# A fused attention and gated-convolution kernel: gate and value weights from one transposed h, token loads for two chunks, finer pieces and a new order

## The chip, the cores and the metric

The kernel runs on one core of a Trainium2 chip. The metric is the device time of one execution in microseconds (us), lower is better. Engines are named as in the profile: PE (TensorE; PEld its weight loads), DVE (VectorE), ACT (ScalarE), POOL (GpSimd), SP (SyncE, which here issues nearly all DMAs).

## What is computed

Two functions in a row, on x of 4 batches x 12800 tokens x 128 channels, all float32 outside:

```python
def mab(q, kv):
    s = scale * (q @ kv.transpose(0, 2, 1))
    a = softmax(s)              # with 1e-9 added to the sum
    return a @ kv
h = mab(inducing, x)            # 32 rows per batch
y = mab(x, h)                   # every token again: y = p @ h, p is tokens x 32

for k in range(5):              # causal convolution along the tokens, per channel
    gate_pre += conv_w[k] * y_shifted[k]
gate = 1 / (1 + exp(-gate_pre))
out = (gate * (y @ w_val)) @ w_out
```

Since y = p @ h, the kernel never forms y. The gate's sum over taps becomes matmuls of p (32 rows, shifted by k tokens) with the weights h * conv_w[k], and the value branch a matmul of p with h @ w_val. So each batch needs, before its gates, a stationary operand W: 5 tap weights and 1 value weight, each 32 rows (of h) x 128 channels, four times one below the other (for the four strips), in two float16 halves (high, and the rest).

## The kernel before

A batch's 12800 tokens are four strips of 3200, which stand on the four quarters of the 128 partitions. A strip is cut into seven chunks of some 500 tokens (SIZES). The work of a batch is a chain of stages:

- load_xt loads a chunk with channels on the partitions (xt). load_xk loads it with tokens on the partitions and a column of ones (xk). In batch 0 make_xk makes the xk of every chunk (MADE) on chip instead: PE transposes blocks of 128 x 128 (L315), ACT or DVE evicts them (L112, L114).
- s1 (L335): scores against the inducing rows; DVE evicts them with a running maximum (L351). gmax takes the maximum over the strips (L363, L387, four operations of 32 partitions at L373, on POOL or DVE). e1: exp on ACT (L395), transposition on DVE (L400). h (L419): the sum over tokens on PE, gathered in H (L436 to L440). prep (L454 to L462): h divided by its sum, with channels on the partitions: hT, 128 x 32.
- prep2 and prep3 make W: the conv taps times hT on POOL with channels on the partitions (cg at L487, wf at L488), halves by ACT and POOL (L492, L493), the value row h @ w_val on PE (L782) and its halves on DVE (L508, L509); then 24 small PE transposes for each half (L527), which put each piece of 32 rows into its quarter, and a copy of 768 columns by ACT or DVE (L112, L114).
- s2 (L590) and joint: the second scores of one or two chunks (JOINT), transposed by DVE (L601), maximum (L613), subtraction on POOL (L619), exp on ACT (L625), sum and reciprocal on DVE (L631 to L634), scaling on POOL (L642), transposition back (L647), and the halves P1 (ACT, L653) and P2 (POOL, L661).
- visit: the gate matmuls of a chunk (L676) run together with the value matmuls of the chunk before (L685); tanh on ACT (L747), the product on DVE (L756), halves on ACT and POOL (L768, L773); outp (L782) multiplies by w_out, eviction by ACT or DVE (L817, L815), store by SP (L822).

All these are operations of a plan. They are numbered as they are made, and TURN is the order, written out by hand, in which they are issued: each engine runs its own operations in that order, SP its loads and stores too. MOVED lists the operations that go to their other engine, BANK the PSUM bank of each PE tile, FULL the output matmuls that use the whole array. Buffers are rings of BUFS tiles: 10 for xt, 4 for xk; a load waits in SP's queue until its tile is free. The weights come as 64-bit numbers (w64, L187) and are turned into float32 by eleven operations on DVE (L199 to L212).

In TURN, batch 0 begins with the loads of chunk 0, then 1, 2, 4, 3, the weights, 6 and 5. After its hT come s1 of batch 1's first chunks, s2 and W of batch 0, the gates of chunk 0, then s1 and h of batch 1 among the gates of batch 0.

Of the kernel before, what the change touches and what calls it, by code (L numbers as in the profile page):

```python
# [19 lines left out]
P = 128  # L20
# [64 lines left out]
def tile_kernel(ctx: ExitStack, tc: tile.TileContext, xt, xk, indT_in, w64, out):  # L85
# [71 lines left out]
    def f_const():  # L157
# [3 lines left out]
        ident = const.tile([P, P], F16, name="ident")  # L161
        make_identity(nc, ident)
# [6 lines left out]
        c_.update(ident=ident, identf=identf, pick=pick)  # L169
# [186 lines left out]
    def gmax(b, g):  # L356
# [109 lines left out]
    def prep2(b):  # L466

        key, w2, gmx, vmx = ("ps", "pv", b), ("w2", b), ("gmx", b), ("vmx", b)
        wf, cg = ("wf", b), ("cg", b)
# [5 lines left out]

        def g0():
            gm = sb(pb, gmx, [P, 1])
# [4 lines left out]
            st["gs", b] = gs  # L482

        i = op("DVE", g0, [ix["hT", b], iw], [gmx], [("hT", b)])
# [6 lines left out]
        ig = op("POOL", g1, [i], [wf, cg], [("hT", b)])  # L491
        ih = op("ACT", lambda: S.copy(sb(pw, w2, [P, 2, TAPS + 1, M], F16)[:, 0, :TAPS], st[wf]), [ig], [w2], [wf])  # L492
        il = op("POOL", lambda: G.tensor_tensor(st[w2][:, 1, :TAPS], st[wf], st[w2][:, 0, :TAPS], ALU.subtract),  # L493
                [ih], [], [wf, w2])

        def g2():
# [5 lines left out]
            st["vs", b] = vs  # L502

        i = op("DVE", g2, [i4], [vmx], [key])
# [6 lines left out]
        iv = op("DVE", g3, [i, ih], [], [key, w2])  # L511
        ix["w2", b] = [[ih, iv], [il, iv]]
# [6 lines left out]

    def prep3(b, e):  # L520
        key, w2, W = ("ps", "wt", b, e), ("w2", b), ("W", b)

        def f6():
            t = pt(key).bitcast(F16)[:, :(TAPS + 1) * P].rearrange("p (k c) -> p k c", c=P)
            for q in range(TAPS + 1):
                for r in range(R):
                    T.transpose(t[32 * r:32 * r + 32, q, :], st[w2][:, e, q, :], c_["ident"])  # L527

        i6 = PE(f6, ix[w2][e], [key], [w2], "strips")

        def f7(j=len(plan.ops)):
            if e == 0:
                sb(pb, W, [P, 2, TAPS + 1, P], F16)
            copy(j, st[W][:, e], st[key].bitcast(F16)[:, :(TAPS + 1) * P].rearrange("p (k c) -> p k c", c=P))

        i7 = op("DVE" if e == 0 else "ACT", f7, [i6] + ([ix[W]] if e else []), [W] * (1 - e), [key] + [W] * e,
                alt="ACT" if e == 0 else "DVE")
        ix[W] = ix["W", b, e] = i7
# [462 lines left out]
```

## Time and profile before

| | |
|---|---|
| three runs | 280.59, 278.68, 280.46 us; median 280.46 |
| the profiled execution | 278.53 us, its span 276.4 us |
| PE busy | 95% of the span |
| DVE, ACT, POOL busy | 82%, 71%, 70% |
| DMA | 73.48 MB, mean 266 GB/s |

The profile is of one execution. The span runs from its first to its last instruction; the time of the execution is a little longer. A busy PE is not PE at its peak, since the ends of pipelined matmuls are modelled.

### The profile page before, as it was taken

What the parts mean: (1) busy time and instruction counts of PE and PEld (TensorE: products, weight loads), DVE (VectorE), ACT (ScalarE), POOL (GpSimd) and SP (SyncE); (2) the same over time, 40 slices, a digit from 0 to 9 for tenths busy, and PEclk for the clock granted to TensorE, in tenths of its full rate; (3) what the DMA queues carried; (4) which work ended last, traced back from release to release, by engine and by line L of the source; (5) the groups of instructions that cost most, each with busy time, mean ns of one, the idle gap of its engine ahead of it and who ended that gap; (6) DMA issues with size and microseconds to landing.
All of it is one profiled execution on the core that took longest, in us unless ns stands there. A gap on an engine that the chain in (4) does not pass through costs nothing.

```text
span 276.4 us, 10872 instructions
## 1 busy us (share of the span) xinstructions
PE 263.7 (95%) x4655; PEld 142.3 (51%) x4655; DVE 227.6 (82%) x441; ACT 196.2 (71%) x257; POOL 194.4 (70%) x152
## 2 busy tenths in 40 slices
PE   8989987999999999999999999999999999999993
PEld 4567634766434473475454356656353445443551
DVE  0688899989999977979999799869979997785680
ACT  2547248696588897875877877858878697887764
POOL 1011068976768895985799739876998898997691
PEclk9999999999999999999999999999999999999999
DMA  7999699799989889659989997633134143344467
GB/s 223 408 408 385 224 409 407 262 364 407 348 275 384 314 284 411 263 198 359 365 272 398 329 384 231 256 129 143 58 114 161 64 169 121 115 162 168 154 231 274
DMA packets 30255, 73.48 MB, mean 266 GB/s; under 512 B 3456, under 2 KB 12800, under 8 KB 30208
## 3 DMA queue, kind: packets, MB, share of 16 engines
q1 hardware_dynamic: 30064, 72.79, 71.9%
q8 instruction: 36, 0.59, 0.9%
q14 instruction: 11, 0.09, 0.1%
q10 hardware_dynamic: 144, 0.02, 0.0%
HBM read 46.57 MB, written 26.21 MB: 263 GB/s over the span
## 4 chain that ended last, share of the span: by engine, by line
PE 57%; DVE 16%; DMA 12%; ACT 4%; issue 4%; POOL 3%; SPq 1%; DVEq 0%; ACTq 0%; POOLq 0%
PE banks L676 20%; PE banks L782 17%; PE banks L419 6%; PE banks L590 5%; DMA xt<-in_xt_dram 4%; PE banks L685 4%; DVE tg L756 4%; PE banks L335 3%; DMA raw<-in_w_dram 3%; DMA xk<-in_xk_dram 2%; DMA out_dram<-os 2%; PE banks L315 2%; DVE e L601 2%; ACT os L817 2%; DVE os L815 2%
## 5 line engine op out<-in xcount | busy, mean ns | idle before, releaser
L773 POOL TENSOR_TENSOR gl<-tg,gh 128x1024 f16<-128x1024 f32 (+4 forms) x54 | 106.2, 1972 | 26.3 <-PE banks L782 12.5
L676 PE MATMUL banks<-P,W 32*128 32x512 f16 (+5 forms) x1680 | 105.5, 352 | 1.3 <-ACT W L112 1.0
L676 PEld LDWEIGHTS <-W 32*128 32x128 f16 x1680 | 54.3, 92 | 38.2 <-issue 8.6
L747 ACT ACTIVATE tg<-banks,gsc 128x1024 f32<-128x1024 f32 (+5 forms) x56 | 55.3, 1018 | 22.6 <-PE banks L676 21.4
L756 DVE SCALAR_TENSOR_TENSOR tg<-tg,banks 128x1024 f32<-128x1024 f32 (+5 forms) x56 | 60.5, 1096 | 5.7 <-PE banks L685 4.9
L782 PE MATMUL banks<-gh,wo 128*32 128x448 f16 (+6 forms) x642 | 61.6, 359 | 0.8 <-DVE tg L756 0.6
L768 ACT CAST gh<-tg 128x1024 f16<-128x1024 f32 (+4 forms) x54 | 52.0, 969 | 10.3 <-DVE tg L756 9.3
L782 PEld LDWEIGHTS <-wo 128*32 128x32 f16 (+1 forms) x963 | 31.8, 97 | 38.5 <-issue 14.8
L685 PE MATMUL banks<-P,W 32*128 32x512 f16 (+5 forms) x336 | 41.7, 353 | 2.3 <-ACT tg L747 1.5
L815 DVE TENSOR_SCALAR os<-banks,osc 128x448 f32<-128x448 f32 (+4 forms) x49 | 32.4, 688 | 11.0 <-PE banks L782 9.5
L782 PE MATMUL banks<-gl,wo 128*32 128x448 f16 (+7 forms) x321 | 40.2, 358 | 0.0
L817 ACT ACTIVATE os<-banks,osc 128x512 f32<-128x512 f32 (+4 forms) x57 | 34.9, 646 | 7.5 <-PE banks L782 6.1
L642 POOL TENSOR_TENSOR e<-e,z 128x1024 f32<-128x1024 f32 (+7 forms) x17 | 25.0, 1468 | 7.1 <-ACT tg L747 2.2
L661 POOL TENSOR_TENSOR P<-pt,P 128x1024 f16<-128x1024 f32 (+7 forms) x17 | 27.9, 1640 | 1.8 <-ACT P L653 1.7
L619 POOL TENSOR_TENSOR e<-e,m 128x1024 f32<-128x1024 f32 (+7 forms) x17 | 24.9, 1470 | 5.4 <-DVE m L613 4.8
L419 PE MATMUL banks<-xk,et 128*32 128x129 f32 x800 | 26.0, 274 | 0.3 <-DVE et L400 0.3
L419 PEld LDWEIGHTS banks<-xk,et 128*32 128x32 f32 x800 | 23.1, 110 | 5.9 <-issue 3.0
L335 PE MATMUL banks<-xt,indT 128*32 128x512 f32 (+5 forms) x224 | 25.1, 557 | 0.0
L590 PE MATMUL banks<-xt,hT 128*32 128x512 f32 (+5 forms) x224 | 24.4, 553 | 0.6 <-ACT tg L747 0.5
L351 DVE TENSOR_SCALAR_CACHE_REDUCE ss<-banks 128x1024 f32<-128x1024 f32 (+8 forms) x17 | 15.9, 933 | 8.6 <-PE banks L335 8.4
L685 PEld LDWEIGHTS <-W 32*128 32x128 f16 x336 | 14.2, 92 | 14.1 <-issue 11.6
L395 ACT ACTIVATE ss<-ss,ng 128x1024 f32<-128x1024 f32 (+8 forms) x17 | 15.5, 922 | 7.0 <-DVE ng L373 6.7
(98 smaller groups left out, 254.4 us busy)
## 6 DMA issues: line engine op xcount, KB each, us to landing
xt<-in_xt_dram SPq DMA_DIRECT2D x28, 512.0 KB, 8.1
xk<-in_xk_dram SPq DMA_DIRECT2D x25, 451.5 KB, 6.8
xt<-in_xt_dram SPq DMA_DIRECT2D x23, 448.0 KB, 7.6
out_dram<-os SPq DMA_DIRECT2D x36, 256.0 KB, 2.9
out_dram<-os SPq DMA_DIRECT2D x40, 224.0 KB, 2.6
xk<-in_xk_dram SPq DMA_DIRECT2D x15, 516.0 KB, 7.0
out_dram<-os SPq DMA_DIRECT2D x20, 240.0 KB, 2.7
out_dram<-os SPq DMA_DIRECT2D x4, 208.0 KB, 4.9
```

What stands on the lines that cost most here:

```text
L335: T.matmul(s[32 * r:32 * r + 32, at:at + n], c_["indT"], st[xkey][:, o:o + n // 32, r, :], start=True, stop=True)
L419: T.matmul(t[32 * s:32 * s + 32, :P + 1], st[et][:, at + 32 * i:at + 32 * i + 32], st[xs[c][0]][:, xs[c][1] + i, :], start=j < R, stop=j > ...
L590: T.matmul(s[32 * r:32 * r + 32, at:at + n], st["hT", b], st[xkey][:, m:m + n // 32, r, :], start=True, stop=True)
L676: T.matmul(two(("ps", "g", b, c, r // 2))[:, r % 2, :n], st["W", b][q, w, k, :], st[("P1", "P2")[e]][q, o:o + n], start=u == 0, stop=u == ...
L685: T.matmul(two(("ps", "v", b, c, r // 2))[:, r % 2, :n], st["W", b][q, w, TAPS, :], st[("P1", "P2")[e]][q, o:o + n], start=u == 0, stop=u ...
L747: S.activation(t[:, :, :n], two(("ps", "g", b, c, p))[:, :, :n], AF.Tanh, scale=st["gsc", b])
L756: V.scalar_tensor_tensor(t, t, 1.0, two(("ps", "v", b, c, p))[:, :, :n], ALU.add, ALU.mult)
L768: S.copy(sb(pw, g1, [P, 2, 512], F16)[:, :, :n], st[tg][:, :, :n])
L773: on(j).tensor_tensor(sb(pw, g2, [P, 2, 512], F16)[:, :, :n], st[tg][:, :, :n], st[g1][:, :, :n], ALU.subtract)
L782: T.matmul(t[q], w[:, q], x, start=j == 0, stop=j == len(terms) - 1)
L815: V.tensor_scalar(o, a, st["osc", b], None, ALU.mult)
L817: S.activation(o, a, AF.Copy, scale=st["osc", b])
```

## The change

- **Weights.** g0 (DVE) also writes hn: hT scaled and repeated four times along the columns, 128 x 128. One PE transpose (tg) turns it, so that h stands on 4 x 32 partitions with channels in the columns. g1 (DVE) multiplies it by cwB, the conv taps spread over all partitions, 640 columns from PSUM; ACT casts the high half straight into W (gh), POOL subtracts for the low half (gl). The value row goes the same way: pn, transpose tv, a copy of 128 columns by ACT, the low half by DVE (g3). cwB is made once: 5 PE transposes of broadcast columns of conv_w, and one ACT copy. prep3 with its 48 small transposes and its copies is gone, and the float16 identity.
- **Batch 0's tokens.** MADE holds five chunks: chunks 5 and 6 of batch 0 come as xk by DMA, 1.06 MB each. GROUPS and PAIRS handle chunks 5 and 6 apart: one more maximum.
- **Pieces.** JOINT of batch 0 cuts chunks 1 and 2 into two pieces each (192 and 224, 256 and 256 columns a strip); a chunk's gates wait for all its pieces.
- **to_strips** writes the strip maximum in three operations instead of four.
- **Order.** TURN, MOVED, BANK and FULL are new. Loads of batch 0 now begin with the first halves of chunks 2 and 3, then 0, 1, the weights, the second halves, 4, 5 and 6, batch 1's first xt, and the token tiles of 5 and 6. The weights' first DVE operation stands ahead of the first s1's eviction. On PE, batch 1's first s1 precedes the last two h of batch 0, batch 1's first h precedes chunk 0's gates and its second precedes chunk 1's gates. In the pieces' order the second of chunk 1 goes first, and the second of chunk 2 is done ahead of the first of chunk 1. Of 10 and 11 maxima, 2 and 7 run on POOL.

```diff
-            for r in range(R):
-                on(j).tensor_scalar(st[ng][32 * r:32 * r + 32, g:g + 1], st[m1][:M, 1:], st[m1][M:2 * M, 1:], -SCALE,
-                                    ALU.max, ALU.mult)
+            to_strips(on(j), st[ng][:, g:g + 1], st[m1], -SCALE)
...
+    def to_strips(e, t, m, by):
+
+        for q in range(2):
+            e.tensor_scalar(t[M * q:M * q + M], m[:M, 1:2], m[M:2 * M, 1:2], by, ALU.max, ALU.mult)
+        e.tensor_copy(t[2 * M:], t[:2 * M])
...
+        def rows(key, x):
+            T.transpose(pt(key)[:, :P], st[x], c_["identf"])
...
+            V.tensor_scalar(sb(pw, hn, [P, P]).rearrange("p (r j) -> p r j", r=R), st["hT", b][:, None, :].broadcast_to([P, R, M]),
+                            gs, None, ALU.mult)
...
         def g1():
-            G.tensor_scalar(sb(pw, cg, [P, TAPS]), c_["cwT"], st["gs", b], 1.0, ALU.mult, ALU.mult)
-            G.tensor_tensor(sb(pw, wf, [P, TAPS, M]), st["hT", b][:, None, :].broadcast_to([P, TAPS, M]),
-                            st[cg][:, :, None].broadcast_to([P, TAPS, M]), ALU.mult)
+            t = sb(pw, wf, [P, 1024])[:, :TAPS * P].rearrange("p (k c) -> p k c", c=P)
+            V.tensor_tensor(t, st[gk][:, None, :P].broadcast_to([P, TAPS, P]), c_["cwB"], ALU.mult)
...
+        def gh():
+            S.copy(st[W][:, 0, :TAPS], st[wf][:, :TAPS * P].rearrange("p (k c) -> p k c", c=P))
...
+        def gl():
+            G.tensor_tensor(st[W][:, 1, :TAPS], st[wf][:, :TAPS * P].rearrange("p (k c) -> p k c", c=P), st[W][:, 0, :TAPS],
+                            ALU.subtract)
...
+            V.tensor_scalar(sb(pw, pn, [P, P]).rearrange("p (r j) -> p r j", r=R), st[key][:, None, :M].broadcast_to([P, R, M]),
+                            vs, None, ALU.mult)
...
+        iv = op("ACT", lambda: S.copy(st[W][:, 0, TAPS], st[vk][:, :P]), [it, i0], [], [vk, W])
 
         def g3():
-            w, p, vs = st[w2], st[key][:, :M], st["vs", b]
-            V.tensor_scalar(w[:, 0, TAPS], p, vs, None, ALU.mult)
-            V.scalar_tensor_tensor(w[:, 1, TAPS], p, vs, w[:, 0, TAPS], ALU.mult, ALU.subtract)
+            V.tensor_tensor(st[W][:, 1, TAPS], st[vk][:, :P], st[W][:, 0, TAPS], ALU.subtract)
...
-    def prep3(b, e):
-        key, w2, W = ("ps", "wt", b, e), ("w2", b), ("W", b)
-
-        def f6():
-            t = pt(key).bitcast(F16)[:, :(TAPS + 1) * P].rearrange("p (k c) -> p k c", c=P)
-            for q in range(TAPS + 1):
-                for r in range(R):
-                    T.transpose(t[32 * r:32 * r + 32, q, :], st[w2][:, e, q, :], c_["ident"])
...
-        cs = JOINT[b][g]
-        ns = [wid(b, c) for c in cs]
+        ps = [(q, 0, wid(b, q) // 32) if isinstance(q, int) else q for q in JOINT[b][g]]
+        cs = [q[0] for q in ps]
+        ns = [32 * (q[2] - q[1]) for q in ps]
...
-                if ix["P", b, c] not in deps:
-                    deps.append(ix["P", b, c])
+                    deps += ix["W", b]
+                deps += [i for i in ix["P", b, c] if i not in deps]
...
+    def cw_tp():
+        t = pt(("ps", "cw"))
+        for k in range(TAPS):
+            T.transpose(t[:, P * k:P * k + P], c_["cwT"][:, k:k + 1].broadcast_to([P, P]), c_["identf"])
...
-GROUPS = [[[0, 1], [2], [3, 4], [5, 6]], [[0, 1, 2], [3, 4, 5, 6]], [[0, 1, 2], [3, 4, 5, 6]], [[0, 1, 2], [3, 4, 5, 6]]]
-PAIRS = [[[0], [1], [2], [3, 4], [5, 6]]] + [[[0], [1, 2], [3, 4], [5, 6]]] * 3
+GROUPS = [[[0, 1], [2], [3, 4], [5], [6]], [[0, 1, 2], [3, 4, 5, 6]], [[0, 1, 2], [3, 4, 5, 6]], [[0, 1, 2], [3, 4, 5, 6]]]
+PAIRS = [[[0], [1], [2], [3, 4], [5], [6]]] + [[[0], [1, 2], [3, 4], [5, 6]]] * 3
 SUMS = [[[c] for c in range(7)]] + [[[0], [1, 2], [3, 4], [5, 6]]] * 3
-JOINT = [[[0], [1], [2], [3, 4], [5, 6]]] + [[[0], [1, 2], [3, 4], [5, 6]]] * 3
-MADE = set(range(7))
+JOINT = [[[0], [(1, 0, 6)], [(1, 6, 13)], [(2, 0, 8)], [(2, 8, 16)], [3, 4], [5, 6]]] + [[[0], [1, 2], [3, 4], [5, 6]]] * 3
+MADE = set(range(5))
...
 TURN = [
...
```

## Rows read from the trace of the kernel before

**Rows 1.** The page, part 1: engine, busy us, share of the span, instructions.

```profile
PE 263.7 (95%) x4655; PEld 142.3 (51%) x4655; DVE 227.6 (82%) x441; ACT 196.2 (71%) x257; POOL 194.4 (70%) x152
```

**Rows 2.** Stretches: us; busy of PE, PEld, DVE, ACT, POOL (instructions); clock, DMA share, GB/s.

```profile
0.00:6.90 6.90, 5.73 (x23) 2.77 (x23) 0.65 (x3) 1.49 (x2) 1.32 (x12) 1.00 0.73 222
6.90:27.60 20.70, 19.34 (x215) 13.16 (x212) 15.57 (x48) 12.26 (x17) 2.25 (x8) 1.00 1.01 401
27.60:34.50 6.90, 6.38 (x180) 4.40 (x178) 6.05 (x18) 1.91 (x3) 0.27 (x1) 1.00 0.66 225
...
30.00:44.50 14.50, 11.21 (x268) 5.86 (x262) 13.49 (x46) 5.35 (x10) 7.25 (x15) 1.00 1.01 383
...
62.00:262.00 200.00, 198.03 (x3526) 100.82 (x3523) 172.88 (x304) 152.94 (x194) 160.64 (x99) 1.00 0.67 244
```

**Rows 3.** The chain that ended last: start us, us, what it ran over.

```profile
19.33 2.84 PE banks L315 x24
22.17 1.85 PE banks L335 x16
...
28.00 3.85 PE banks L419 x128
...
33.23 0.20 DVE hT L462
...
43.47 0.98 POOL P L661
...
44.49 0.27 PE banks L676
...
53.19 1.15 PE banks L782 x45
```

**Rows 4.** Timeline, 32 to 43 us: start, us, engine, line, operation [idle before].

```profile
32.62 0.19 DVE L460 TENSOR_SCALAR zr<-banks 128x32 f32<-128x32 f32 x1
...
40.72 1.63 PE L676 MATMUL banks<-P,W 32*128 32x224 f16 x60 [0.98 <-ACT W L112]
...
41.59 0.61 DVE L647 STREAM_TRANSPOSE pt<-e 128x416 f32<-128x416 f32 x1
...
42.03 1.35 POOL L373 TENSOR_SCALAR ng<-m 32x1 f32<-32x1 f32 x4
```

**Rows 5.** Timeline of SP's DMA issues, 8 to 32 us.

```profile
8.05 11.18 SPq L263 DMA_DIRECT2D xt<-in_xt_dram  x10
29.20 2.82 SPq L283 DMA_DIRECT2D xk<-in_xk_dram  x6
```

**Rows 6.** The chain again, one half of a batch's small weight transposes.

```profile
97.02 0.34 PE banks L527 x24
```

**Rows 7.** Timeline of PE, 0 to 9 us.

```profile
1.17 3.60 PE L831 MATMUL banks<-zero 128*128 128x512 f16 x8 [1.17 <-DVE warm L159]
...
4.56 1.70 PE L315 MATMUL banks<-identf,xt 128*128 128x128 f32 x7
...
6.19 0.90 PE L335 MATMUL banks<-xt,indT 128*32 128x224 f32 x8
...
8.07 0.91 PE L335 MATMUL banks<-xt,indT 128*32 128x416 f32 x8
```

**Rows 8.** Groups by shape: line, engine, operation, shapes, count | busy us, mean ns | idle.

```profile
L756 DVE SCALAR_TENSOR_TENSOR tg<-tg,banks 128x1024 f32<-128x1024 f32 x20 | 23.8, 1209 | 2.4 <-PE banks L685 2.0 <-ACT gh L768 0.4
...
L756 DVE SCALAR_TENSOR_TENSOR tg<-tg,banks 128x448 f32<-128x448 f32 x2 | 1.2, 614 | 0.1
...
L440 DVE TENSOR_TENSOR H<-H,banks 128x129 f32<-128x129 f32 x9 | 2.5, 283 | 3.8 <-PE banks L419 2.7 <-ACT os L817 0.6 <-ACT gh L768 0.2
...
L631 DVE TENSOR_REDUCE z<-e 128x16 f32<-128x512 f32 x2 | 1.4, 679 | 0.0
...
L631 DVE TENSOR_REDUCE z<-e 128x8 f32<-128x256 f32 x1 | 0.4, 408 | 0.0
...
L211 DVE TENSOR_SCALAR ul<-raw 128x261 int32<-128x261 int32 x1 | 0.3, 292 | 0.0
```

More of the change, by code (lines that the diff above doesn't have):

```diff
@@ L481, in g0, with tg @@
             V.reciprocal(gs, gm)
-            st["gs", b] = gs
-        i = op("DVE", g0, [ix["hT", b], iw], [gmx], [("hT", b)])
-        def g1():
-            G.tensor_scalar(sb(pw, cg, [P, TAPS]), c_["cwT"], st["gs", b], 1.0, ALU.mult, ALU.mult)
-            G.tensor_tensor(sb(pw, wf, [P, TAPS, M]), st["hT", b][:, None, :].broadcast_to([P, TAPS, M]),
-                            st[cg][:, :, None].broadcast_to([P, TAPS, M]), ALU.mult)
[L491 to L494, printed above, removed]
+            V.tensor_scalar(sb(pw, hn, [P, P]).rearrange("p (r j) -> p r j", r=R), st["hT", b][:, None, :].broadcast_to([P, R, M]),
+                            gs, None, ALU.mult)
+        i0 = op("DVE", g0, [ix["hT", b], iw], [gmx, hn, W], [("hT", b)])
+        def tg():
+            rows(gk, hn)
+        i = PE(tg, [i0, i_const], [gk], [hn])
+        def g1():
+            t = sb(pw, wf, [P, 1024])[:, :TAPS * P].rearrange("p (k c) -> p k c", c=P)
+            V.tensor_tensor(t, st[gk][:, None, :P].broadcast_to([P, TAPS, P]), c_["cwB"], ALU.mult)
+        i = op("DVE", g1, [i, i_cw], [wf], [gk])
+        def gh():
+            S.copy(st[W][:, 0, :TAPS], st[wf][:, :TAPS * P].rearrange("p (k c) -> p k c", c=P))
+        ih = op("ACT", gh, [i], [], [wf, W])
+        def gl():
+            G.tensor_tensor(st[W][:, 1, :TAPS], st[wf][:, :TAPS * P].rearrange("p (k c) -> p k c", c=P), st[W][:, 0, :TAPS],
+                            ALU.subtract)
+        il = op("POOL", gl, [ih], [], [wf, W])
         def g2():
@@ L553, in f1 @@
             over_strips(on(j), st[qm], TINY)
-            for r in range(R):
-                on(j).tensor_scalar(u[32 * r:32 * r + 32], st[qm][:M, 1:2], st[qm][M:2 * M, 1:2], 1.0 / SO, ALU.max, ALU.mult)
+            to_strips(on(j), u, st[qm], 1.0 / SO)
             on(j).tensor_scalar(sb(pb, ("osc", b), [P, 1]), u, 0.5 / SP, None, ALU.mult)
@@ L585, in f @@
             s = pt(key)
-            for c, n, at in zip(cs, ns, places(ns)):
+            for (c, i0, i1), n, at in zip(ps, ns, places(ns)):
                 xkey, m = xt_of(b, c)
-                m -= HALO // 32 if c == 0 else 0
+                m += i0 - (HALO // 32 if c == 0 else 0)
                 for r in range(R):
@@ L603, in s2, with joint @@
         ix["tin", b, g] = op("DVE", tin, [i], [ek], [key], size=sum(ns))
-        joint(b, g, cs)
-    def joint(b, g, cs):
-        n = sum(wid(b, c) for c in cs)
+        joint(b, g, ps)
+    def joint(b, g, ps):
+        n = sum(32 * (q[2] - q[1]) for q in ps)
+        c0, i0 = ps[0][:2]
+        first = c0 == 0 and i0 == 0
         nb = n // 32
@@ L634, in sm @@
             V.reciprocal(z[:, 0, :nb], w[:, 0])
-            if cs[0] == 0:
+            if first:
                 V.memset(z[:M, 0, :1], 0.0)
@@ L663, in joint @@
         i = op("POOL", lo, [i], [], [qk], size=n)
-        for c in cs:
-            ix["P", b, c] = i
+        for c, _, _ in ps:
+            ix.setdefault(("P", b, c), []).append(i)
     taps = [(k, e, 0) for k in range(TAPS) for e in range(2)] + [(k, 0, 1) for k in range(TAPS)]
@@ L835, in tile_kernel, with cw_ev @@
     iw = weights(op("SP", f_wload, [], [("tg", "w", 0)], size=P * K64 * 8))
+    def cw_tp():
+        t = pt(("ps", "cw"))
+        for k in range(TAPS):
+            T.transpose(t[:, P * k:P * k + P], c_["cwT"][:, k:k + 1].broadcast_to([P, P]), c_["identf"])
+    def cw_ev():
+        c_["cwB"] = const.tile([P, TAPS, P], F32, name="cwB")
+        S.copy(c_["cwB"], st["ps", "cw"][:, :TAPS * P].rearrange("p (k c) -> p k c", c=P))
+    i_cw = op("ACT", cw_ev, [PE(cw_tp, [iw, i_const], [("ps", "cw")], size=TAPS, wide=2)], [], [("ps", "cw")])
     for b in range(B):
@@ L855, in tile_kernel @@
         prep2(b)
-        prep3(b, 0)
-        prep3(b, 1)
         prep_out(b)
```

39 lines of the change are left out of this document (16 added, 23 removed), and 128 rows, old and new, of tables (BANK, MOVED, TURN).

## The prediction

> **What bounds the kernel now.** The page's first part [rows 1] says TensorE: PE is busy 263.7 us of a span of 276.4. Busy time there is not peak rate, so I split the span by stage [rows 2]. From 62 to 262 us PE has 198.0 of 200 us, while DVE has 172.9 and POOL 160.6: in that stretch an instruction taken off PE shortens the kernel. From 30 to 44.5 us it is not so: PE 11.2, DVE 13.5 of 14.5. The start is a third thing: from 6.9 to 27.6 us DMA moves 401 GB/s at a share of 1.01, then drops to 225 GB/s.
>
> So there are three stages with three limits: loading, then DVE, then PE to the end. The chain of waits [rows 3] shows the seams. Around 20 to 32 us it runs over PE: 24 transposes in 2.84 us, s1, h, and at last 128 h matmuls in 3.85 us to 31.85. hT is done at 33.43. From there the chain is almost all DVE, until POOL writes chunk 1's low half of P (43.47 to 44.45) and the gate matmuls of chunk 1 follow at 44.49. The gates of chunk 0 ran at 40.72 for 1.63 us [rows 4], so PE had nothing to do for about two microseconds ahead of 44.49. SP issues nothing from 19.23 to 29.20 us [rows 5]: the token tiles of batch 1 wait for buffers that the h matmuls free.
>
> **The change, part by part.**
>
> *PE instructions.* 32 of the 100 block transposes go (chunks 5 and 6): at 2.84/24 = 0.118 us [rows 3], 3.8 us. The 48 small weight transposes of each batch go: 24 take 0.34 us [rows 6], so 0.68 per batch and 2.7 us in all. Added are 5 transposes of spread conv_w and 2 per batch, 13 in all, 1.5 us at 0.118. Net 5.0 us less PE work. Only batches 1 to 3 lie in the PE stage, with 3 x (0.68 - 0.24) = 1.3 us; that part I count in full. The other 3.7 us lie in the first two stages, where DMA and DVE end last.
>
> *Loading.* Chunks 5 and 6 come twice, as xt and as tokens: 2 x 16 x 66,048 B = 2.11 MB more. Before, all that is issued up to 19.23 us (9.83 MB by the loads' sizes) is in by 27.6 us: 222 GB/s x 6.9 us + 401 x 20.7 gives the same 9.83 MB [rows 2]. In the new order the token tile of chunk 6 ends 9.98 MB: batch 0's xt 6.62, w 0.27, batch 1's first xt 0.98, two token tiles 2.11. It takes the buffer of chunk 2, whose h stands well ahead in PE's order, so the queue need not stop: moved by 28.0 us. How far a wait's end lies behind the bytes is bounded by the first s1 of chunk 1: 1.38 MB stand up to its last load, which by the same rates are moved by 6.5 us, and it started at 8.07 [rows 7]; so 0 to 1.6 us, and I take 1.1. Then come 16 blocks of h (3.85/4 = 0.96 us) and, as before, 1.6 us from the last h to hT (31.85 to 33.43): hT at 30.5 to 32.1, I take 31.6, 1.8 us earlier. PE, with 3.8 us of transposes less, could be there before the tile, so it partly waits them away. The new order also puts halves of chunks 2 and 3 ahead of 0 and 1: up to the second half of chunk 1 stand 2.43 MB, not 1.38; at 401 GB/s its s1 starts 2.6 us after 8.07, near 10.7. That costs nothing while the last token tile ends this stage; without that cover it would cost up to those 2.6 us.
>
> *Weights.* hn and pn (128 columns) are no dearer than L211's 261 in 0.29 [rows 8]: 0.2 us each. g1 multiplies 640 columns from PSUM; L756 takes 0.614 for 448 and 1.209 for 1024, so 0.81. The new g3 has 128 columns, as L440 with 129: 0.28. The two operations of the old g3 go; on 32 columns they are below L211, 0.24 each. In batch 0 DVE gains 1.0 us. ACT and POOL get one long cast and subtraction for several short ones. In batches 1 to 3 I count all this at nothing: PE's stage hides it (DVE has 27 of 200 us free, POOL 39). In batch 0 the weights must be there for the first gates, ahead of which PE's order now puts batch 1's first h; that h hides them. Uncovered, they would hold the first gates alone, which have no follower but chunk 1's.
>
> The Trainium skill (VectorE: DVE Perf Modes, "Why PSUM operands drop a tier") says that a PSUM operand keeps fp32 at one element a cycle. L756's slope in rows 8, 1.03 ns a column, is that rate; by that page's clock g1's 640 columns are an estimated 0.67 us before the fixed part, so the sum stays the same by the page.
>
> *Chunks 1 and 2 of batch 0 in two pieces.* A split gives five DVE operations a second fixed part; from 256 against 512 columns [rows 8], 2 x 0.408 - 0.679 = 0.14 for a reduction; I put 0.14 to 0.3 for each of the other four, of which one has small followers that double as well: about 0.95 us a split, at least 0.7. What matters is the queue. Before, DVE goes from 32.62 (first row of hT) to 42.20 (chunk 1 transposed back) [rows 4], 9.6 us. In the new order: +0.95 for the split of chunk 1 and +1.0 for the weights; ahead of that point now stand the transposes of batch 1's first scores (1408 columns, by L756's slope 1.7), an H copy (0.28), a whole piece of chunk 2 (five operations on 256 columns, at L631's 0.41 each 2.1) and the transposition of one more piece (0.41); off it go the reduction of batch 1's first s1 and the transposition of all of chunk 2 (0.68 each, by L631 at 512). Sum 14.7. Starting 0.8 ahead of hT, at 30.8, it ends at 45.5. Behind it, as before, stand ACT's copy and POOL's subtraction, 2.25 us then (42.20 to 44.45), with the same maxima of batch 1 between. Chunk 1's gates start near 47.8, 3.3 us later than 44.49.
>
> In that time PE does work that it did afterwards before: h of batch 1's first three chunks, 86 matmuls at 3.85/128, 2.6 us. Net late at that seam: 0.7 us, from -0.5 (DVE operations overlap a little) to +1.5. Queued behind these gates on PE are s1 of batch 1 and the first output matmuls, whose evictions feed SP's stores. The next seam is chunk 2's gates, at 54.3 before, when the output matmuls of chunk 0 were done (45 in 1.15 us [rows 3]). They need chunk 2's second piece, behind two 1024-column operations and two gate products on DVE: I put them with 0 to 1.5 us more delay and three of four output groups still to do; what PE has in their place fills most of it, so 0.1 us more.
>
> *One strip operation less* in each of 11 maxima and 4 scales: 0.34 us on POOL, where four take 1.35 [rows 4]; but five maxima move from DVE to POOL. Counted at nothing, since they lie beside PE's work; where POOL does one ahead of a P half, as at 42.03, it would be about 1 us.
>
> *Sum* against the profiled run, 278.53 us (span 276.4 and 2.1 around it): -1.3 (PE stage), +0.7, +0.1, and 0 for the tail, whose order changes little: -0.5, between -2.5 and +2. That makes 278.0. The three runs have median 280.46, 1.9 above the profiled run, and one at 278.68, so the result may stand at either level: 280.0 from the median. I say 279.0.
>
> **Rivals.**
>
> A: PE's savings count in full. If DVE's queue is shorter than I add up, or PE's new order fills both seams, all 5.0 us come off: 273.5 in the profiled run. For it: PE is the busiest engine of the page. Against: DVE's 13.5 of 14.5 us where 3.7 of the 5.0 lie.
>
> B: slower. One mechanism: DVE's queue between 31 and 48 us. PE's order puts batch 1's first h ahead of even chunk 0's gates, and that h waits for a DVE transpose deep in the queue. Every microsecond that DVE waits there for ACT or POOL (POOL now has the 640-column subtraction between chunk 0's subtraction and its scaling) delays both seams one for one. With 4 us of waits: 282. It decides from about 3 us on; before, DVE stood idle for 1.0 us there.
>
> C: loading does not hold 401 GB/s. At 375 the last token tile is 1.5 us later, and hT with it: 279.5 to 281.5 by the level. For it: only the 222 GB/s of the first 6.9 us, where the queue had just begun.
>
> D: TensorE's clock. The first 7 transposes take 1.70 us, 0.24 each, against 0.118 later; 8 matmuls of 224 columns take 0.90, as long as 8 of 416 at 8.07 [rows 7]. Rows 2 put the granted clock up to 6.9 us at 1.00, but by these durations PE ran at the lower level (1.2 GHz) until about 7 us, after 3.6 us of warm-up and those. In the new order 16 to 20 transposes alone follow the warm-up, then a wait of about 2 us for chunk 1. If PE stays at the lower level through the first s1, some 2.5 us of its work take twice as long; with 0.7 us of slack against the last tile that is 1.8 us: 279.8 to 281.8 by the level. Against: after 24 transposes in a row at 19.33 the s1 that follows runs at full rate (16 in 1.85 us). The Trainium skill (TensorE: Matmul & The Clock Gate, "Part 4: PE-mode transpose") says that transposes do not engage the full clock; rows 3 show only that they do not lose it.
>
> **How the numbers follow.** Forecast 0.42, A 0.28, B 0.20, C 0.05, D 0.05. About 1% is what a measurement of this kernel can tell from no change: below 277.7 or above 283.3. The forecast's own range is 276.0 to 282.0. Faster by over 1%: all of A and a sixth of the forecast, 0.35. Slower: four fifths of B and a little of C and D, 0.18. Within: 0.47. The range reaches to A's time and to B's between the two levels: 273.5 to 283.0.
>
> **What would show it.** Right: hT near 31.6, chunk 1's gates near 47.8 with batch 1's h ahead of them, chunk 2's near 55, DVE over 9 of 10 us between 31 and 50; the stage from 62 us on shorter by about 1.3. Wrong: a load rate under 390 GB/s before 28 us, hT after 33, PE without a pause between 31 and 56 (A), DVE waiting over 3 us there (B), or a stage after 62 us that changes by more than 2 us: then the new order later on, which I have counted at nothing, decides.

## The result and the profile after

| | before | after |
|---|---|---|
| median of 13 runs each | 278.96 us (277.99 to 280.59) | 282.61 us (281.18 to 284.62) |
| the profiled execution | 278.53, span 276.4 | 282.89, span 279.9 |

The ratio is 1.0125, with a 95% interval of 1.0096 to 1.0155: slower by 3.65 us, by over 1%. The prediction said 279.0, and put most of its chance on no change or faster. The time lies in its range; its sign is that of rival B, and "slower by over 1%" had been given 0.18.

PE's line in the page's first part, after (engine, busy us, share, instructions), to be read against [rows 1]:

```profile
PE 260.9 (93%) x4433; PEld 136.5 (49%) x4433; DVE 225.8 (81%) x427; ACT 194.6 (70%) x262; POOL 200.5 (72%) x168
```

PE is busy 2.8 us less and stands idle 19.0 us of the span instead of 12.7. Where it does so is read from the stretches of after, with the columns of [rows 2]:

```profile
0.00:6.90 6.90, 5.13 (x19) 2.41 (x20) 1.59 (x4) 1.49 (x2) 0.88 (x10) 1.00 0.75 243
6.90:27.60 20.70, 17.46 (x255) 11.64 (x257) 13.68 (x45) 11.62 (x18) 3.37 (x13) 1.00 1.03 411
27.60:34.50 6.90, 5.09 (x120) 3.28 (x109) 5.19 (x20) 1.16 (x3) 0.00 (x0) 1.00 1.03 404
...
30.00:44.50 14.50, 10.77 (x207) 5.88 (x206) 12.61 (x50) 5.40 (x11) 7.04 (x14) 1.00 1.03 406
31.00:50.00 19.00, 13.69 (x284) 8.28 (x287) 17.04 (x57) 7.63 (x16) 10.82 (x22) 1.00 1.03 406
62.00:262.00 200.00, 197.34 (x3380) 99.77 (x3376) 170.97 (x281) 153.62 (x197) 166.95 (x111) 1.00 0.69 242
```

Up to 34.5 us PE is busy for 27.68 us (5.13 + 17.46 + 5.09) against 31.45 before: the 3.8 us of transposes are gone, and it waits all of them away, since the loads, 411 GB/s without a break, still end the stage. From 62 to 262 us PE's line looks as before (197.34 against 198.03), yet the work in it has moved: the same milestone comes later. The table takes milestones of the two profiled executions, each the start of the first matmuls named.

| milestone | before | after | later by |
|---|---|---|---|
| hT of batch 0 (end) | 33.43 | 33.12 | -0.31 |
| gates of chunk 0 | 40.72 | 43.05 | 2.33 |
| gates of chunk 1 | 44.49 (two of the 60 matmuls had run at 43.90) | 48.73 | 4.24 (h of batch 1 now ahead of them) |
| gates of chunk 2 | 54.28 | 56.06 | 1.78 |
| gates of chunk 3 | 61.77 | 65.38 | 3.61 (2.65 for the same work: two more groups of output matmuls, 0.96, stand ahead) |
| first gates of batch 3 | 219.80 | 224.44 | 4.64 |
| last values | 266.79 | 270.15 | 3.36 |
| span | 276.4 | 279.9 | 3.5 |

So about 2.65 us are lost in the opening and another 2.0 from there to 220 us, where the prediction had counted on 1.3 us less. At the gates of chunk 4 of batch 3 the kernel is still 4.64 late (247.36 against 252.00); 1.1 come back between there and the end.

The chain of waits of after, between 20 and 34 us (start us, us, what), stands beside [rows 3]:

```profile
20.44 1.06 PE banks L421 x32
21.56 0.33 SPq L281
21.93 7.92 DMA xk<-in_xk_dram
29.89 0.32 PE banks L421 x5
30.21 0.34 DVE w L210
30.56 0.12 issue
30.68 0.36 DVE H L440
31.08 0.26 PE banks L456 x5
31.34 0.62 issue
31.95 0.33 PE banks L456 x11
32.31 0.20 DVE zr L462
32.54 0.37 DVE zr L463
32.92 0.20 DVE hT L464
```

The chain goes over the last token tile, which lands at 29.85, then over a step of the float weights on DVE (L210) that stands ahead of H, and over a pause of 0.62 us between the five and the eleven matmuls of f3, whose cause the profile does not show ("issue"). From the last h (30.54) to hT it takes 2.58 us, where it took 1.6.

The second place is batches 1 and 3. hn, on DVE at L488, in the timeline of after (start us, us, engine, line, operation), first its own summary (duration min/median/max in ns), then its neighbours on POOL in batch 1 and batch 3:

```profile
L488 DVE TENSOR_SCALAR hn<-hT,gs x4: 286/628/1157, 33.8 to 203.4; 128x128 f32<-128x128 f32 x4
...
78.02 2.14 POOL L667 TENSOR_TENSOR P<-pt,P 128x1024 f16<-128x1024 f32 x1 [2.35 <-ACT P L659]
79.27 0.97 DVE L488 TENSOR_SCALAR hn<-hT,gs 128x128 f32<-128x128 f32 x1
...
202.43 2.01 POOL L778 TENSOR_TENSOR gl<-tg,gh 128x960 f16<-128x960 f32 x1 [1.64 <-ACT gh L773]
203.37 1.16 DVE L488 TENSOR_SCALAR hn<-hT,gs 128x128 f32<-128x128 f32 x1
```

The same instruction, four times: 0.29 us in batch 0, where POOL does nothing beside it, and in batch 2 (at 137.65, POOL idle from 137.31 to 141.17); 0.97 in batch 1 and 1.16 in batch 3, each begun inside an instruction of POOL. There its end lies 0.08 us behind the end of POOL's instruction (80.24 behind 80.16, 204.52 behind 204.44). The chain of after at 203 us shows that in batch 3 this is on the path: DVE's next product for the gates starts when hn is done. For batch 1 the chain shows no such thing; around 79 us it runs over PE.

```profile
203.37 0.03 DVE hn L488
203.40 1.04 issue
204.44 1.07 DVE tg L761
```

### The profile page after: what moved, and what is told of

Same layout as the page of the kernel before. It is cut to its first block, busy times and chain, and to the rows that moved or that the text cites. A ratio compares the mean times of both kernels' runs of the same rounds, so it can differ in the third digit from the quotient of the medians.

```text
span 279.9 us, 10452 instructions
## 1 busy us (share of the span) xinstructions
PE 260.9 (93%) x4433; PEld 136.5 (49%) x4433; DVE 225.8 (81%) x427; ACT 194.6 (70%) x262; POOL 200.5 (72%) x168
## 4 chain that ended last, share of the span: by engine, by line
PE 72%; DVE 12%; DMA 5%; issue 4%; ACT 3%; SPq 1%; POOL 0%; DVEq 0%; ACTq 0%; POOLq 0%
PE banks L682 26%; PE banks L787 19%; PE banks L421 7%; PE banks L333 7%; PE banks L691 6%; PE banks L594 5%; DMA xk<-in_xk_dram 3%; DMA xt<-in_xt_dram 2%; DVE tg L761 2%; DVE os L820 2%; PE banks L313 1%; DVE e L605 1%; DVE pt L653 1%; ACT tg L752 1%; ACT ss L397 1%
## 5 line engine op out<-in xcount | busy, mean ns | idle before, releaser
L787 PE MATMUL banks<-gh,wo 128*32 128x448 f16 (+7 forms) x624 | 62.1, 360 | 0.3 <-DVE tg L761 0.3
L787 PEld LDWEIGHTS <-wo 128*32 128x32 f16 (+1 forms) x936 | 33.1, 97 | 38.2 <-issue 15.6
L822 ACT ACTIVATE os<-banks,osc 128x448 f32<-128x448 f32 (+5 forms) x57 | 36.0, 647 | 12.6 <-PE banks L787 11.7
L625 POOL TENSOR_TENSOR e<-e,m 128x1024 f32<-128x1024 f32 (+8 forms) x19 | 25.3, 1333 | 19.2 <-DVE m L619 17.7
L820 DVE TENSOR_SCALAR os<-banks,osc 128x512 f32<-128x512 f32 (+5 forms) x49 | 31.7, 685 | 7.6 <-PE banks L787 6.4
L667 POOL TENSOR_TENSOR P<-pt,P 128x1024 f16<-128x1024 f32 (+8 forms) x19 | 28.2, 1485 | 2.8 <-ACT P L659 2.6
L648 POOL TENSOR_TENSOR e<-e,z 128x1024 f32<-128x1024 f32 (+8 forms) x19 | 25.3, 1334 | 0.6 <-DVE z L640 0.4
L594 PE MATMUL banks<-xt,hT 128*32 128x512 f32 (+6 forms) x240 | 24.6, 528 | 0.5 <-DVE hT L464 0.4
L659 ACT CAST P<-pt 128x1024 f16<-128x1024 f32 (+8 forms) x19 | 14.4, 756 | 9.5 <-DVE pt L653 9.4
L605 DVE STREAM_TRANSPOSE e<-banks 128x1024 f32<-128x1024 f32 (+8 forms) x19 | 16.7, 881 | 4.4 <-PE banks L594 4.3
```

Source lines behind the costliest of these rows:

```text
L594: T.matmul(s[32 * r:32 * r + 32, at:at + n], st["hT", b], st[xkey][:, m:m + n // 32, r, :], start=True, stop=True)
L787: T.matmul(t[q], w[:, q], x, start=j == 0, stop=j == len(terms) - 1)
L820: V.tensor_scalar(o, a, st["osc", b], None, ALU.mult)
L822: S.activation(o, a, AF.Copy, scale=st["osc", b])
```

## The experiments

The question is where 3.65 us come from when PE has less to do. The theories, as the expectations name or number them: the opening (the loads, hT, DVE's queue; in it, that loads issued behind the last token tile slow that tile), the new order of the later batches, and the weights' new operations, whose cost I had put at 1.0 us on DVE in batch 0 and at nothing after.

**One part at a time, in hybrids of the two orders.** The first four kernels take the new weights in each. In w_alone all else is as before. In old_open_new_rest the opening is the old one up to the gates of chunk 3 and the order behind it the new one; in new_open_old_rest it is the other way round; new_loads_old_rest has the new order up to f3 alone. Where the order is the old one, the weights' new operations stand in the place of the old ones. In all four the product with the taps has a buffer of its own, and z two buffers instead of three.

```diff
# w_alone, against the changed kernel; TURN is that of before with the new weights' operations put in
-MADE = set(range(5))
+MADE = set(range(7))
-GROUPS, PAIRS: batch 0 ends with [5], [6];  JOINT: batch 0 has (1, 0, 6), (1, 6, 13), (2, 0, 8), (2, 8, 16)
+GROUPS, PAIRS: batch 0 ends with [5, 6];    JOINT: batch 0 has [1], [2]
```

> The new weights (and the maximum in three operations) alone: all seven token tiles of batch 0 made on chip, whole chunks, and the order of before, with the new operations put where the old ones of the weights stood. The product with the taps has a buffer of its own here, which the changed kernel shares with the transposed pieces. Theory 1 (the time is lost in the opening of the changed kernel, up to some 65 us, and the weights give what they take off TensorE): 1.3 to 2.7 us under before, 276 to 277.7. Theory 2 (the new order of batches 1 to 3 is what costs): the same here. Theory 3 (the new form of the weights costs, by its work on VectorE and GpSimd): at before's time or over it, 279 to 281.

> As the run with the weights alone, but from the gates of chunk 3 of batch 0 on (61.8 us in before) everything is issued in the order of the changed kernel. Theory 1: within 0.5 us of the weights alone. Theory 2: 2 to 3 us over the weights alone, since between 65 and 222 us the changed kernel falls back by 2 us for the same work although 1.3 us of work are gone. Theory 3: as the weights alone, 279 to 281.

> The opening of the changed kernel (its loads, its pieces, its order up to the gates of chunk 3) and from there on the order of before. Theory 1: as slow as the changed kernel, 281.5 to 283. Theory 2: 279 to 280.5, the 2 to 3 us of the later order back. Theory 3: as slow as the changed kernel.

> The changed kernel's loads and its order up to the last sum over tokens of batch 0 (chunks 5 and 6 loaded in tokens), then whole chunks and the order of before. Theory 1 splits here: if the pieces and the order around the first gates cost, this is 1 to 3 us faster than the changed kernel, 279.5 to 281.5, with the gates of chunk 1 near 44.5 us as before; if the loads alone cost, it is as slow as the changed kernel. Theory 2: 277 to 279. Theory 3: 280 to 282.

Measured: w_alone 295.4 us, ratio 1.057 (1.051 to 1.063); old_open_new_rest 284.43, 1.020 (1.013 to 1.026); new_open_old_rest 295.2, 1.055 (1.049 to 1.061); new_loads_old_rest 296.64, 1.059 (1.053 to 1.065). Three of the four are 15 to 17 us slower, far outside what any theory gave: those with the later batches in the old order. In w_alone's timeline POOL's low half of the weights (1.41 us, at 38.02) stood ahead of chunk 0's subtraction, ready since 36.45. PE stood idle for other operations of the weights too: 1.90 us from 95 us for a product whose low half stood behind that of the weights, 1.64 at 156 for the product with the taps, and 0.89 at 140 and 2.06 at 207 for DVE's product with the gates, which stood behind hn; hn took 2.12 and 2.04 us there. The four don't tell the parts apart, then, and the theories stay open. They tell that a few operations of 0.3 to 1.4 us put into wrong places of in-order queues cost more than all that was in dispute.

**The weights alone, placed with care.** w_placed is w_alone with the operations of the weights and of prep_out (what follows a batch's value row, up to its scales) moved to places where DVE and POOL do not hold others up; after_reordered and before_reordered are the changed kernel and the kernel before with an order found by a search over a model of the queues (durations from the two traces).

> The run with the weights alone again (all seven token tiles made on chip, whole chunks, the order of before for everything else), but only the operations of the weights and of prep_out are put elsewhere in the order: the low half's subtraction on GpSimd no longer stands ahead of chunk 0's subtraction, where it held the first gates until 43.4 us. Theory 3 (the new form of the weights costs by itself, wherever it stands): again far over before, 290 or more. Theory 1 and a fourth theory (each part is worth what it takes off TensorE, but the order decides whether it is got: an operation in the wrong place of a queue costs more than it is long): 277 to 279, 1 to 2 us under before.

> The changed kernel with all its parts; only the order, the engine of the operations that can go to either, and the banks are other ones, searched for with a model of the queues that is fed with the durations of the two traces. Theory 4 (the order decides): 274 to 278, faster than both kernels, with the idle time of TensorE between 27 and 62 us shorter than the 6 us of the changed kernel. Theory 1 in its narrow form (the loads and the pieces themselves cost): 280 or more, as no order gives it back.

> The kernel before with no part of the change; only its order, engines and banks are searched for in the same way and for as long. Theory 4 with parts that are worth something: 275 to 278, behind the changed kernel in its searched order by about 1 us, less than the 5 us of TensorE work between them, since most of that lies where loads and VectorE set the end. If the parts are worth nothing: the same as the changed kernel in its searched order, or faster. If the order of before cannot be bettered: 279.

Measured: w_placed 282.48 us, ratio 1.009 (1.006 to 1.013): the new weights, with their operations and those of prep_out in new places and no other part of the change, are as slow as all of it (282.61). Both searched orders failed: after_reordered 297.3, 1.057 (1.048 to 1.065), before_reordered 285.99, 1.022 (1.017 to 1.027). In after_reordered's profile PE is idle for 27.9 us, and the granted clock falls to 0.50 twice for 6.8 us (from 37 and from 105 us).

In w_placed one place stands out. The bulk of chunk 5's gates of batch 0 comes 3.67 us late (85.97 against 82.30) where chunk 4's began 1.6 late, after an hn of 1.62 us at 80.03, and in batch 3 hn is at its longest (timeline of w_placed):

```profile
201.94 3.99 POOL L778 TENSOR_TENSOR gl<-tg,gh 128x960 f16<-128x960 f32 x2 [0.77 <-PE banks L787]
205.90 1.99 DVE L488 TENSOR_SCALAR hn<-hT,gs 128x128 f32<-128x128 f32 x1
205.90 1.91 POOL L625 TENSOR_TENSOR e<-e,m 128x1024 f32<-128x1024 f32 x1
```

hn begins with POOL's instruction and ends 0.08 us behind it: 1.99 us for what takes 0.29.

**The loads.** loads_later is the changed kernel with one of batch 1's token tiles ahead of two of its xt, so that those two come later (one execution).

```diff
 load_xk(b=0, c=6)
+load_xk(b=1, c=0)
 load_xt(b=1, c=1)
 load_xt(b=1, c=2)
-load_xk(b=1, c=0)
```

> The changed kernel with one load moved: the first token tile of batch 1, which has to wait for a buffer until about 27 us, stands ahead of batch 1's second and third channel tiles in the queue of SyncE, so that these two are issued after it instead of at 22.4 to 24.7 us. If transfers that are issued later share the rate with those ahead of them (theory 1a), the token tile of chunk 6 is in about 1 us earlier than at 29.85 us, and hT stands near 32; the total may still grow by 1 to 2 us, since batch 1's scores then wait for their tiles. If the queue is served in order, the token tile is in at 29.85 as before and only the scores are late.

Measured: 285.03 us. The last token tile landed at 29.43 instead of 29.85, but the loads ahead of it were as much earlier in that execution (the token tile before it 28.09 instead of 28.54), and it landed 1.3 us behind that one in both; so what stands behind it in the queue doesn't slow it. Loads landed in the order of their issue. hT was done at 31.87, 1.75 us after the last h. PE then waited for batch 1's third xt, which landed at 37.79, and ran at a granted clock of 0.50 from 37.3 to 44.1. An hT 1.25 us earlier did not help that kernel.

**The weights' work of the later batches.** weights_once leaves out the making of W in batches 1 to 3, which use batch 0's. gl_twice does POOL's subtraction for the low half of the gate weights twice there.

```diff
# gl_twice
+            for _ in range(2 if b else 1):
-            G.tensor_tensor(st[W][:, 1, :TAPS], ..., st[W][:, 0, :TAPS], ALU.subtract)
+                G.tensor_tensor(st[W][:, 1, :TAPS], ..., st[W][:, 0, :TAPS], ALU.subtract)
```

> The changed kernel in its own order, with the weights' work of batches 1 to 3 left out: hn, pn, their two transposes, the product with the taps, the cast, the subtraction and the value row are done for batch 0 only, and batches 1 to 3 multiply by batch 0's weights (so only their times mean anything). Taken off each later batch: 0.24 us of TensorE, some 2 us of VectorE, 1.4 us of GpSimd and 1 us of ScalarE. Theory 5 (the weights' work in batches 1 to 3, counted at nothing in the prediction, is not hidden: VectorE and GpSimd serve it in the middle of queues for which TensorE waits): 2.5 to 4 us under the changed kernel, 278.5 to 280. Theory 2 (the new order of batches 1 to 3 costs, the work itself is covered): only TensorE's 0.7 us back, 281.5 to 282.2.

> The changed kernel with the subtraction for the low half of the weights done twice in batches 1 to 3 (the same result): 1.4 us more of GpSimd in each, 4.2 us in all, while GpSimd stands idle for 33 of 200 us in the stage from 62 us on. Theory 5: 1.5 to 3 us over the changed kernel. Theory 2 and the prediction (GpSimd's work is hidden by TensorE's stage): the same time within 0.4 us.

Measured: weights_once 280.26 us, ratio 1.004 (1.001 to 1.007), 2.35 under the changed kernel. PE's share of it is 0.24 a batch by the prediction's count, 0.7 (PE's line shows 0.5: 260.4 against 260.9); the medians leave at least 1.6 for the operations that I counted at nothing. The two profiled executions leave less, and say where: weights_once stands 0.84 us ahead already at chunk 3's gates of batch 0, before anything is left out, 0.71 at chunk 4's of batch 2 (198.53 against 199.24), and 1.88 at batch 3's first gates (222.56 against 224.44). So in this pair batches 1 and 2 gave nothing on balance, and the stretch with the making of batch 3's weights 1.2 us. gl_twice 285.21, 1.022 (1.015 to 1.028): 4.2 us more of POOL's work cost 2.6. POOL's idle time in that stage (33 of 200 us) is no cover either.

**hn on ScalarE.** One operation of four moves from DVE to ACT, in the changed kernel, where nothing else moves, and in w_placed, where the operations beside hn also change places with their neighbours in DVE's queue (in batch 1 behind two others, in batch 3 ahead of three).

```diff
# hn_on_scalar; weights_hn_scalar has the same edit in w_placed, and a few places in the order besides
-            V.tensor_scalar(sb(pw, hn, [P, P])..., st["hT", b][:, None, :].broadcast_to([P, R, M]), gs, None, ALU.mult)
+        def gn():
+            S.activation(sb(pw, hn, [P, P])..., st["hT", b][:, None, :].broadcast_to([P, R, M]), AF.Copy, scale=gs)
+        i1 = op("ACT", gn, [i0], [hn], [("hT", b)])
-        i = PE(tg, [i0, i_const], [gk], [hn])
+        i = PE(tg, [i1, i_const], [gk], [hn])
```

> The changed kernel with one operation moved: hn, which VectorE multiplies from one tile of SBUF to another, goes to ScalarE. In batch 0 it took 0.29 us, in batches 1 and 3 0.97 and 1.16 us, and there it ended with the instruction that GpSimd had begun before it (80.24 beside 80.16, 204.52 beside 204.44). If VectorE waits there for GpSimd and TensorE for VectorE (part of theory 5): 0.5 to 1.5 us under the changed kernel. If VectorE has the time (theory 2): the same time within 0.4 us.

> As w_placed (the new weights alone, in the order of the kernel before), but hn is made on ScalarE instead of VectorE. Theory hn (a scaling of 128 columns on VectorE waits until GpSimd's instruction beside it ends, and w_placed paid 1.3 and 2.0 us for it in batches 1 and 3): w_placed's 282.5 us falls by 2 to 3 us, to 279.5 to 280.5, level with the kernel before. Rival order (the weights' other operations, in whatever place, hold DVE's and POOL's queues): it falls by less than 1 us, 281.5 or more. It also tells what loads, pieces and the new order add together: the changed kernel with hn on ScalarE took 280.48; if this one is at 279.5 they add 0.5 to 1 us.

Measured: hn_on_scalar 280.48 us, ratio 1.005 (1.002 to 1.009), 2.1 under the changed kernel; in core 0's span the medians are 1.55 apart (278.65 against 280.2). weights_hn_scalar 279.87, 1.003 (1.000 to 1.005), 2.6 under w_placed, which with those other moves isn't hn's place alone. The summary of hn in weights_hn_scalar, and its place in hn_on_scalar beside the POOL instruction that had held it up:

```profile
L493 ACT ACTIVATE hn<-hT,gs x4: 391/400/402, 34.0 to 201.5; 128x128 f32<-128x128 f32 x4
...
78.83 2.14 POOL L672 TENSOR_TENSOR P<-pt,P 128x1024 f16<-128x1024 f32 x1 [2.34 <-ACT P L664]
79.66 0.39 ACT L493 ACTIVATE hn<-hT,gs 128x128 f32<-128x128 f32 x1
```

On ACT it takes 0.40 us always, with POOL's 2.14 us beside it. Where the time comes from is read from the two profiled executions of after and hn_on_scalar, whose orders are the same but for hn: first after, then hn_on_scalar.

```profile
204.44 1.07 DVE L761 SCALAR_TENSOR_TENSOR tg<-tg,banks 128x896 f32<-128x896 f32 x1
205.57 0.58 PE L787 MATMUL banks<-gh,wo 128*128 128x480 f16 x2 [0.28 <-DVE tg L761]
```

```profile
80.21 0.19 DVE L522 TENSOR_REDUCE vmx<-banks 128x1 f32<-128x32 f32 x1 [0.76 <-PE banks L792]
203.51 1.09 DVE L766 SCALAR_TENSOR_TENSOR tg<-tg,banks 128x896 f32<-128x896 f32 x1
```

hn_on_scalar stands 0.81 us behind at chunk 3's gates of batch 0, with a drop of the granted clock to 0.50 from 32.6 to 36.0 us, and 0.25 behind at 79 us (78.99 against 79.24). Over batch 1's hn that stays (0.24 at chunk 5's gates, 83.64 against 83.88): DVE, free of hn, waits 0.76 us for PE instead. Over batch 2's hn, which nothing had held up, it stays too (0.26 at chunk 4's gates, 199.24 against 199.50). Over batch 3's it turns into a lead of 0.81 at batch 3's first gates (224.44 against 223.63). So in this pair batch 3's hn is worth 1.1 us and the other three nothing. What the rest of the 2.1 is, if it is more than the spread of the executions, is not shown.

The milestones of weights_hn_scalar read in the later batches as the prediction thought they would: 2.06 us late at chunk 3's gates of batch 0 (61.95 against 64.01), then 1.52 at chunk 2's of batch 1, 0.89 at its last chunk, 0.05 at batch 3's first gates and 0.43 ahead at its last (262.07 against 261.64). PE has 48 small transposes less in each batch there; that the 2.5 us are theirs alone is not shown. Its last store took 4.05 us from issue to landing where that of before took 2.95, and the span is 0.8 longer.

**The pieces.** whole_pieces puts chunks 1 and 2 back whole, in the place of one of their pieces.

```diff
-JOINT = [[[0], [(1, 0, 6)], [(1, 6, 13)], [(2, 0, 8)], [(2, 8, 16)], [3, 4], [5, 6]]] + ...
+JOINT = [[[0], [1], [2], [3, 4], [5, 6]]] + ...
```

> The changed kernel with chunks 1 and 2 of batch 0 whole again: each is done where its first piece stood in the order (the second of chunk 1, the second of chunk 2), and the other pieces' operations are gone, about 0.95 us of VectorE a chunk. If the pieces cost as the prediction put it, the gates of chunk 1 start 0.5 to 1 us earlier than at 48.7 us and the total falls by up to 1 us. If the pieces pay by letting the next engine start earlier, the gates of chunk 1 start later than 49 us, and the total rises by 1 us or more.

Measured: 285.82 us, ratio 1.023 (1.015 to 1.031), 3.2 over the changed kernel. With the whole chunks the new order is slower, then. That the pieces themselves pay is not shown: the granted clock fell to 0.50 at 11.1 and at 48.6 us in its profile, so a part of the 3.2 may be that, and the rest of the order was made for the pieces.

**hT earlier.** clear_before_ht is hn_on_scalar with DVE's queue cleared ahead of hT.

```diff
# DVE's order, up to hT of batch 0
+weights (L210), cmax
 h.acc(g=2)
 h.acc(g=3)
-s1.g (batch 1)
-weights (L210)
 h.acc(g=4)
-cmax
+s1.g (batch 1)
 f4 (hT)
```

> The changed kernel with hn on ScalarE, and VectorE's queue cleared between the last h and hT of batch 0: the last operations on the weights stand ahead of the two last H copies, batch 1's first reduction of scores behind them. Theory opening (each part of a microsecond that hT is late is paid at the end): hT 0.3 to 0.5 us earlier, 280.0 us against 280.48. Rival (VectorE's later queue sets the opening): no change within 0.3 us.

Measured: 280.67 us, ratio 1.007 (1.004 to 1.010), no change against 280.48. hT was done at 32.35 instead of 33.19, and chunk 0's gates started at 42.19 (after: 43.05). Then comes this, PE's timeline of clear_before_ht and of after, and the stretches of clear_before_ht:

```profile
45.86 2.62 PE L421 MATMUL banks<-xk,et 128*32 128x129 f32 x60 [2.05 <-ACT tg L757]
```

```profile
46.73 1.95 PE L421 MATMUL banks<-xk,et 128*32 128x129 f32 x60 [2.05 <-ACT tg L752]
```

```profile
42.20:47.00 4.80, 2.75 (x104) 2.53 (x106) 4.63 (x16) 2.18 (x6) 3.07 (x6) 1.00 1.03 406
47.00:50.40 3.40, 3.40 (x56) 2.71 (x50) 2.62 (x4) 0.42 (x1) 2.49 (x8) 0.50 1.03 406
```

The same 60 matmuls after the same pause of 2.05 us: here the clock falls to the lower level (1.2 GHz) for 3.4 us, there it does not. By chunk 1's next matmuls the lead is gone (49.09 against 49.13), and from chunk 2's gates on this kernel stands 0.04 us behind after. hn_on_scalar has such a drop too, at 32.6. So whether an earlier hT is worth its 0.84 us can't be read from these runs. That the profiled span of clear_before_ht is 1.3 us longer than that of after is no sign against it: its last store took 4.3 us to land where after's took 2.8.

## Why the prediction was wrong, by its steps

**PE's instructions: right up to hT, too high behind it, and of no use in the opening.** PE was busy 3.8 us less up to 34.5 us and waited it away, as the prediction expected. Rival A fell with that. Over the span it was busy 2.8 us less, not 5.0: behind 34.5 us it was busy 1.0 us more. The new 128 x 128 transposes were put at 0.118 us each; those of hn and pn took 0.27 to 0.33 by the profile, a part of which their neighbours overlap. From 62 to 262 us PE was busy 0.7 us less, where 1.3 was put.

**Loading: the mechanism was right, the term too small.** The rate held (411 GB/s against the 401 of [rows 2]; rival C fell). The token tile landed at 29.85 instead of 29.1, and from the last h to hT it took 2.58 us instead of 1.6, because the step that copied this from [rows 3] did not look at what DVE and PE have in their queues in the new order: a step of the float weights ahead of H, and a pause inside f3 (open in its cause). hT came at 33.12 instead of 31.6, by the prediction's own list a sign that it is wrong ("hT after 33").

**DVE's queue from hT to chunk 1's gates: near.** Predicted 47.8 - 31.6 = 16.2 us, measured 48.73 - 33.12 = 15.6. Of the 1.5 us of hT, 0.9 arrived at chunk 1's gates (48.73 against 47.8) and 1.1 at chunk 2's (56.06 against "about 55"). DVE was busy 17.04 of the 19 us from 31 to 50, just short of the nine tenths listed. Together the opening cost 2.65 us where 0.8 was put. How much of that is hT's stays open: weights_hn_scalar, in the old order and with its hT at 33.28, lost 2.06 us there through the new weights and the places of prep_out, and clear_before_ht does not tell.

**Weights in batches 1 to 3, "counted at nothing, PE's stage hides it": the step that failed.** It had two errors. hn was priced 0.2 us from L211 [rows 8], which ran while POOL had nothing to do (POOL is busy 0.27 of 6.9 us there, [rows 2]); beside POOL it takes 0.97 and 1.16, and 1.62, 0.98 and 1.99 in w_placed's batches 1 to 3. And idle time summed over 200 us (DVE's 27, POOL's 39) is no cover for an operation at one place: DVE runs its queue in order, and what stands behind hn in batch 3 is a chunk's product with the gates, for which PE waits. The weight of the step is measured two ways: 2.35 us for all of the weights' work there (weights_once), 2.1 for hn's place alone (hn_on_scalar); in the profiled executions they are 1.2 and 1.1, both in batch 3. The stage from 62 to 220 us came out 2.0 us longer instead of 1.3 shorter. hn explains 1.1 to 2.1 of these 3.3 us; the rest stays open.

The Trainium skill (SBUF — State Buffer, "SBUF: two separate sides") states that VectorE and GpSimd share one pair of ports as an exclusive lock: an instruction of GpSimd, or one of VectorE that runs in a 2-port mode or has two inputs in SBUF, holds it from start to end, and the second to come is blocked and not slowed in proportion. Whether hn is an instruction of that kind the traces don't say, but they agree in what decides: hn waits until POOL's instruction ends, with 0.08 to 0.09 us between the two ends in all 21 instances that were stretched, and on ACT it doesn't wait. They show no full 0.29 us behind that end, which a strict reading would give.

**New order, counted at nothing: open.** By its own list ("a stage after 62 us that changes by more than 2 us: then the new order ... decides") the prediction pointed here. hn_on_scalar, with loads, pieces and order, is 0.6 us above weights_hn_scalar, which has none of them; the two intervals overlap. The profiled executions do not say that the sum is so small: PE ends 2.2 us later in hn_on_scalar (273.67 against 271.49), which lost 0.8 in the opening by the time of chunk 3's gates, and weights_hn_scalar loses 1.3 against it in its last store (4.05 us to land against 2.77). What the new order alone is worth stays open, since each hybrid of the two orders also put the weights' operations into other places.

**The tail**, put at 0, gave back 1.1 us behind chunk 4 of batch 3; no run looked at why.

**The rivals.** B had the sign, not the mechanism: DVE waited 1.9 us of 14.5 between 30 and 44.5, less than the 3 us from which B decides, and of what the forecast missed the larger part lies later. D did not come: the first s1 after the wait, 8 matmuls of 416 columns, took 0.91 us, as in [rows 7]. That the profiled time is 278.53 and the shown median of three 280.46 was no reason to add 1.0: the median of 13 executions of the kernel before is 278.96.

Put together against the forecast for the profiled execution (278.0, measured 282.89): 1.85 from the opening, 3.3 from batches 1 to 3, -1.1 from the tail, and 0.9 since the time outside the span was 3.0 in this execution where it had been 2.1 before (in other executions of after it is 2.1 too: 281.91 with a span of 279.8). That the range of 273.5 to 283.0 holds the 282.61 is owed to its width, which was set by the rivals' times, and not to the forecast's steps.

No kernel here beats the one before. The best, weights_hn_scalar, is level with it within 0.5%.

## What to carry to other kernels

Read the duration of a new instruction from one of its own form, with GpSimd busy and idle beside it, not from a like shape elsewhere in the trace: hn, a scaling of 128 x 128 from SBUF to SBUF, ran up to seven times as long beside an instruction of POOL, while the other operations of DVE in these traces, several of them from SBUF to SBUF, kept their durations there (the 128 x 1024 transposes of pt 1.23 to 1.25 us beside POOL and without it). If such an instruction stands in a queue ahead of work that PE needs, try it on ScalarE. Idle time summed over a stage hides nothing by itself: name the instruction behind the new one in its queue, and who waits for that. When a load becomes the end of a stage, walk the queues between its landing and the next milestone anew.

## What the runs showed of the hardware

- A scaling of 128 x 128 from SBUF to SBUF (hn) took 0.29 us on DVE with POOL idle, 0.95 (gl_twice) to 2.12 us (w_alone) beside an instruction of POOL, and then ended 0.08 to 0.09 us after it. On ACT it took 0.39 to 0.40 beside such instructions. In w_alone hn began 0.03 us ahead of POOL's instruction (137.77 and 137.80) and was still the one that was held up.
- After some pauses of PE the granted clock was 0.50 (1.2 GHz): from 47.0 to 50.4 us in clear_before_ht, 32.6 to 36.0 in hn_on_scalar, 37.3 to 44.1 in loads_later, and twice for 6.8 us in after_reordered. By an estimate from half the rate, a drop of 3.4 us costs up to 1.7. The same pause of 2.05 us ahead of the same matmuls brought a drop in clear_before_ht and none in after, so the pause alone doesn't tell.
- All 101 loads of after, and of loads_later, landed in the order of their issue on one queue, some 1.28 us for each 512 KB at 410 GB/s; a load put ahead of others did not hasten or slow those ahead of it (loads_later, one execution).
